# Storing two 64 MB gradients from ScalarE's queue, behind VectorE, in place of GpSimd's queue

## The chip, the cores and the metric

The kernel runs on one core of one Trainium2 chip. Its time is device microseconds of that core, from the start of the program to its end. A core has five engines with a queue of instructions each, and each queue runs in order: TensorE (PE; its weight loads are PEld), VectorE (DVE), ScalarE (ACT), GpSimd (POOL) and SyncE (SP). SP, ScalarE and GpSimd can issue DMA transfers between the chip's memory (HBM) and the core's on-chip buffers (SBUF, PSUM); 16 DMA engines carry them out.

## The reference: what is computed

One decode step of a small transformer block with a cache, forward and backward, B = 2 sequences, D = 640, H = 32 heads of width 128, a cache of 4096 positions, all in bfloat16:

```
h   = x + attention(layernorm(x), k_cache, v_cache) @ wo      # softmax over 4096 positions, per head
out = h + relu(layernorm(h) @ w1) @ w2                        # Dff = 1728
gradients of out (with grad_out) to x, k_cache, v_cache, wq, wo, w1, w2
```

k_cache and v_cache are (2, 32, 4096, 128): 64 tiles of 1 MB each, 128 partitions of 8 KB. Their gradients have the same size. For one head (b, h) with scores p (softmax), query q, gradient `go` of the head's output, and `dp` = V go, they are outer products: gV[s, :] = p[s] go and gK[s, :] = p[s] (dp[s] - p.dp) q scale. So 128 MB are written for gK (out_2) and gV (out_3), and V is read twice.

## The kernel before, in words

**Two passes over the heads.** The first pass (`p1_iter`) runs over the 64 heads and reads K and V of each: PE transposes K's tile group by group (`t_ps`, two banks), ScalarE copies each group out (`t_sb`, line 429), PE multiplies it with the query (scores), ScalarE takes the exponential (`ep`, line 524), VectorE weights K by it (`pk`, line 470), and PE forms M = pk' V (line 460). The second pass (`p2_iter`) runs over the heads again in the order `turns` and reads V as `Wt` (twelve V tiles are kept from the first pass): PE transposes it, ScalarE copies, PE forms `dp`; ScalarE scales the rows `rb` (go and q of this head, line 882); VectorE writes gV (two halves, line 844, from `rb` and `pp`), `gsp` from dp (line 858), and gK (two halves, line 844). For 19 heads ScalarE writes the last eight of gV's 32 column groups (line 930). gV and gK are stored by one DMA each: lines 909 and 931 for gV, 899 and 941 for gK. All four issue from GpSimd's queue.

**Steps.** `p2_iter` is a generator; each `next` of it is a step, some five to eight for a head. The main loop (`for n, (i, j) in enumerate(plan)`) takes steps of `p2_iter` between the steps of `p1_iter` while the first pass runs (i is not None; a head of the second pass for every second of the first, from i = 41 on), and later one step after the other, with background work between them (`bg_step`: gradients of the weights, their outer products `ot`, the sums `gxj`). Everything is issued in the order in which Python calls it; there is no other scheduler. Each engine's queue holds its own share of that order.

**Buffers.** 1 MB tiles come from a fixed set of buffers with owners ("ld" for loads, "g" for gK and gV, "f" and "q" for others). `take` gets one, `give` returns it in program order; the next user then waits on the chip for the last reader of the buffer, for a gK or gV that is its store's landing. Loads go out on SP's queue through `pump` as soon as an "ld" buffer has been given.

**Semaphores.** In the built program the DMAs of SP and ScalarE signal eight semaphores in turn, so that each waits for the landing of the eighth before it; the DMAs of GpSimd have eight of their own.

Of the kernel before, what the change touches and what calls it, by code (L numbers as in the profile page):

```python
# [15 lines left out]
def kernel(  # L16
# [20 lines left out]
    nc = tc.nc  # L37
# [402 lines left out]
    def natural(cache, b, h):  # L440
        return cache[b, h].rearrange("(p sc) d -> p sc d", sc=NSC)
# [412 lines left out]
    def score_grad(j, c):  # L854
# [5 lines left out]
            in1=P_bf[:, b * H + h, :, None].to_broadcast([128, NSC, 2]), op0=ALU.add, op1=ALU.mult)  # L860
        return gsp

    def p2_iter(j, busy, act=0, own_gK=False, early=False):

        c = S2[j] if j < NP1 else None
        p = S2.get(j - 1)
        if p is not None:
            bp, hp = turns[j - 1]
            last_dp(j - 1, p)
            gsp = score_grad(j - 1, p)  # L870
        if c is not None:
            b, h = turns[j]
            go = gom[:, h, b, :, :]

            bank = pst([128, 512], FP32, "sps", "dp_ps")
            for k, col in enumerate((goc, qsc)):
                nc.tensor.matmul(bank[:, 128 + k * 128:256 + k * 128],  # L877
                                 lhsT=col[:, h, b:b + 1].to_broadcast([128, 128]), rhs=ident_bf[:],
                                 start=True, stop=True)
            c["dp"] = bank[:, 0:NSC]  # L880
            rb = mats.tile([128, 256], BF16, tag="rb", bufs=3, name="rb")
            nc.scalar.activation(out=rb[:], in_=bank[:, 128:384], func=ACT.Copy, scale=rt[:, b, h:h + 1])  # L882
            pp = small.tile([128, NSC, 2], BF16, tag="pp", bufs=2, name="pp")
            nc.gpsimd.tensor_copy(out=pp[:], in_=P_bf[:, b * H + h, :, None].to_broadcast([128, NSC, 2]))
            c.update(rb=rb, pp=pp)
            if act:
                pa = small.tile([128, 8], FP32, tag="pa", bufs=2, name="pa")
                nc.gpsimd.tensor_copy(out=pa[:], in_=P_bf[:, b * H + h, NSC - act:NSC])
            c["T0"] = pair_transpose(c["W"], 0, busy=busy)
        if p is not None:  # L890
            gK = take("g", [128, NSC, 128], "gK")
            outer_half(gK, p["rb"][:, 128:256], gsp, 0)
        yield
        if early:
            gV = take("g", [128, NSC, 128], "gV")
            outer_half(gV, c["rb"][:, 0:128], c["pp"], 0)
        if p is not None:
            outer_half(gK, p["rb"][:, 128:256], gsp, 1)
            nc.gpsimd.dma_start(out=natural(out_2, bp, hp), in_=gK[:])  # L899
            give(gK)  # L900
            del S2[j - 1]
        yield
        if c is None:
            return
        c["T1"] = pair_transpose(c["W"], 1, busy=busy)
        pair_matvec(c["dp"], c.pop("T0"), 0, go)
        if early:
            outer_half(gV, c["rb"][:, 0:128], c["pp"], 1)
            nc.gpsimd.dma_start(out=natural(out_3, b, h), in_=gV[:])
        yield  # L910
        c["T2"] = pair_transpose(c["W"], 2, busy=busy)
        pair_matvec(c["dp"], c.pop("T1"), 1, go)
        yield
        c["T3"] = pair_transpose(c["W"], 3, busy=busy)
        give(c["W"], "g" if j < H and j != 1 and owned["g"] < 3 else None)
        pair_matvec(c["dp"], c.pop("T2"), 2, go)
        if early:
            give(gV)
            yield
            last_dp(j, c)  # L920
            gsp = score_grad(j, c)
        else:
            gV = take("g", [128, NSC, 128], "gV")
            outer_half(gV, c["rb"][:, 0:128], c["pp"], 0)
            yield
            if own_gK:
                last_dp(j, c)
            outer_half(gV, c["rb"][:, 0:128], c["pp"], 1, act)
            for k in range(act):
                nc.scalar.activation(out=gV[:, NSC - act + k, :], in_=c["rb"][:, 0:128], func=ACT.Copy, scale=pa[:, k:k + 1])  # L930
            nc.gpsimd.dma_start(out=natural(out_3, b, h), in_=gV[:])  # L931
            give(gV)
            if own_gK:
                gsp = score_grad(j, c)
            yield
        if own_gK:
            gK = take("g", [128, NSC, 128], "gK")
            outer_half(gK, c["rb"][:, 128:256], gsp, 0)
            yield
            outer_half(gK, c["rb"][:, 128:256], gsp, 1)  # L940
            nc.gpsimd.dma_start(out=natural(out_2, b, h), in_=gK[:])
            give(gK)
            del S2[j]
            yield

# [267 lines left out]
    def p2_step():  # L1213
        nonlocal g2
        try:
            next(g2)
        except StopIteration:
            g2 = None

    for n, (i, j) in enumerate(plan):  # L1220
        all_go = all(("go", B - 1, h) in done for h in range(H))
        if i is None and plan[n - 1][0] is not None:
            pkp.release()
            big1 = tc.alloc_tile_pool(name="big1", bufs=1)
            for _ in range(2):
                more_home("ld", big1)
            share(ld=KEPT[1] + 4, g=5)
        if all_go and not late[0]:
            wop.release()
            big3 = tc.alloc_tile_pool(name="big3", bufs=1, side="right")  # L1230
            for tag in ("ld", "g", "g", "q", "q", "q"):
                more_home(tag, big3)
        late[0] = all_go
        more = int(late[0])
        if fin is not None and not bg2 and not bg3:
            share(ld=8 + 3 * more, g=7 + 3 * more)
        elif fin is not None and j >= H + KEPT[1] - 1:
            share(ld=5 + more, g=6 + 2 * more, f=3, q=2 + 3 * more)
        if j is not None:
            while g2 is not None:  # L1240
                p2_step()
            if j < NP1:
                bg_until(("go", *turns[j]))
            g2 = p2_iter(j, 0, 8 if i is None and j <= H else 0, i is not None and plan[n + 1][1] is None, j < EARLY)
        if i is None and ("w1", 1) in done and fin is None:
            wts.release()
            fin = tc.alloc_tile_pool(name="fin", bufs=1)
            big2 = tc.alloc_tile_pool(name="big2", bufs=1)
            more_home("f", big2)
            banks.update(sps=[2, 3], o=[4, 5, 6])  # L1250
            bg2.append(("fin", fin_gen(fin)))
            bg3.append(("gx", gx_gen(fin)))
        if i == 12:
            bg.append(("ga", ga_gen()))
        if i == H + 2:
            banks["bc"].insert(0, banks["sps"].pop(0))
        elif i == P2_AT:
            banks["bc"].remove(7)
            banks["sps"].insert(0, banks["bc"][0])
            banks["bc"] = [7]  # L1260
        rate = RATES[0 if i is not None and i <= H + 1 else 1 if j is None and i < P2_AT else
                     2 if i is not None else 3 if j <= H else 4]
        if i is None:
            spread[0] = 2
            at_k[0] = 1
            k = 0
            while g2 is not None:
                p2_step()
                pump()
                slot[0] = int(k in ((1, 3, 5) if j <= H else (1, 4)))  # L1270
                k += 1
                bg_step(0, rate)
                bg_step(1, RATE2 * (0.4 if spreading[0] else 1.0))
                bg_step(2, RATE3)
            continue
        at = MIXED if j is not None else REST
        for k, _ in enumerate(p1_iter(i, i < H + 1, 0)):
            for _ in range(at.get(k, 0)):
                if g2 is not None:
                    p2_step()  # L1280
            if k == 5 and not H + 2 < i < P2_AT + 6:
                a_heads(i)
            pump()

            spread[0] = 1 if i < P2_AT else 2
            at_k[0] = k
            if i >= P2_AT:
                slot[0] = int(k == 6 or (k == 1 and j is not None))
            elif i > H + 1:
                slot[0] = {1: 2, 3: 1, 4: 1, 6: 1}.get(k, 0)  # L1290
            else:
                slot[0] = int(k in (1, 6))
            bg_step(0, rate)
            bg_step(1, 0.0)
        if i is not None and i in (H + 1, NP1 + 1):
            bg.append((f"m{i // H - 1}", middle_gen(i // H - 1)))
    forced[0] = True
    slot[0] = 99
    left = [q for q in (bg, bg3, bg2) if q]
# [38 lines left out]
```

## Time and profile before

| | |
|---|---|
| median of 3 runs | 891.21 us (891.13 to 893.05) |
| profiled execution | 888.48 us, span 886.3 us |
| PE, PEld, DVE, ACT, POOL busy | 738.8, 618.2, 681.3, 498.8, 204.1 us |
| moved | 361.85 MB: 211.11 read, 149.13 written, the rest instructions and the like; mean 408 GB/s |
| gV and gK | 64 stores each of 1024 KB on POOL's queue, median 14.9 and 15.0 us from issue to landing |

The span is from the first to the last instruction. The profile cuts it into 40 slices of 22.16 us, counted here from 0. First pass alone: to about 260 us. Both passes: to about 460. Second pass alone with the rest: to the end. "DMA share" is the busy share of the 16 DMA engines; "landing" is from the issue of a transfer to the semaphore that tells of its completion. The chain is the work that ended last, followed back from the end. A window's line gives its length, the busy time of the engines, the clock granted to PE, the DMA share and GB/s.

### The profile page before, as it was taken

Reading aid. Unit: us, or ns where it says so; the run is one execution under the profiler, and the core shown is the slowest. Engines: PE = TensorE matmul, PEld = TensorE weight load, DVE = VectorE, ACT = ScalarE, POOL = GpSimd, SP = SyncE. Lnnn points to the kernel's source line nnn. Section 1 sums busy time; section 2 is a strip of 40 time slices with the busy share of each in tenths; the row PEclk is TensorE's granted clock in tenths of the full one; section 3 lists DMA queues with packets and bytes.
Section 4 is the critical chain, followed back from the end, with each engine's and each line's share of the span. In section 5 each row is a group of like instructions: output and inputs, shape, how many; then the busy total and the mean of one; then the engine's idle time right before and its main releaser. Section 6 shows DMA issues by size and latency. Waiting matters only on the chain.

```text
span 886.3 us, 24732 instructions
## 1 busy us (share of the span) xinstructions
PE 738.8 (83%) x10143; PEld 618.2 (70%) x10143; DVE 681.3 (77%) x1281; ACT 498.8 (56%) x1292; POOL 204.1 (23%) x358
## 2 busy tenths in 40 slices
PE   4999899999999997988868767787877899867690
PEld 4887788888887886877757656665656667564550
DVE  2666787877788896876778887878788689989861
ACT  1444343446776664654536767777656766545570
POOL 1344433343312010000011332222222111111220
PEclk9999999999999999998995655555566755555555
DMA  9999999999879999999999999999999999999996
GB/s 380 423 420 414 417 409 417 425 423 412 332 295 402 423 423 426 422 426 425 414 398 396 418 421 421 420 413 420 419 416 403 417 425 420 425 425 425 425 424 275
DMA packets 56289, 361.85 MB, mean 408 GB/s; under 512 B 5680, under 2 KB 11760, under 8 KB 15472
## 3 DMA queue, kind: packets, MB, share of 16 engines
q1 hardware_dynamic: 34520, 211.13, 57.8%
q0 software_dynamic: 18432, 134.23, 36.5%
q10 hardware_dynamic: 3224, 14.92, 4.1%
q8 instruction: 80, 1.31, 0.5%
q14 instruction: 33, 0.27, 0.1%
HBM read 211.11 MB, written 149.13 MB: 406 GB/s over the span
## 4 chain that ended last, share of the span: by engine, by line
PE 35%; DMA 34%; DVE 16%; ACT 7%; issue 5%; SPq 0%; POOL 0%; ACTq 0%; POOLq 0%; DVEq 0%
DMA Vt<-in_A_v_cache_dram 15%; PE t_ps L424 14%; DMA out_dram<-gK 11%; PE m_ps L460 9%; DVE gK L844 4%; DVE gV L844 4%; DMA out_dram<-gV 3%; ACT gV L930 3%; PE s_ps L437 3%; DMA wqs<-in_A_wq_dram 3%; DVE pk L470 2%; PE u_ps L498 2%; ACT t_sb L429 2%; PE dp_ps L437 2%; DVE gxj L678 2%
## 5 line engine op out<-in xcount | busy, mean ns | idle before, releaser
L429 ACT COPY t_sb<-t_ps 128x512 f32<-128x512 f32 x479 | 273.1, 587 | 192.4 <-PE t_ps L424 188.6
L437 PEld LDWEIGHTS <-t_sb 128*128 128x128 bf16 x4096 | 178.9, 102 | 63.8 <-ACT t_sb L429 36.2
L424 PE MATMUL t_ps<-ident_f,Wt 128*128 128x128 f32 x832 | 198.6, 389 | 0.9 <-ACT t_sb L429 0.9
L470 DVE TENSOR_TENSOR pk<-Kt,ep 128x2048 bf16<-128x2048 bf16 (+1 forms) x128 | 152.6, 1193 | 47.1 <-ACT ep L524 29.0
L460 PE MATMUL m_ps<-pk,Vt 128*128 128x129 bf16 x2048 | 172.0, 223 | 19.9 <-DMA Vt<-in_A_v_cache_dram 18.8
L844 DVE TENSOR_TENSOR gK<-rb,gsp 128x2048 bf16<-128x2048 bf16 x128 | 153.4, 1227 | 13.3 <-DMA out_dram<-gV 8.5
L460 PEld LDWEIGHTS <-Vt 128*128 128x128 bf16 x2048 | 125.6, 99 | 50.2 <-issue 28.4
L424 PEld LDWEIGHTS t_ps<-ident_f,Wt 128*128 128x128 f32 x832 | 138.2, 202 | 31.9 <-issue 25.2
L424 PE MATMUL t_ps<-ident_f,Kt 128*128 128x128 f32 x1024 | 156.0, 286 | 2.5 <-DMA Kt<-in_A_k_cache_dram 1.9
L844 DVE TENSOR_TENSOR gV<-rb,pp 128x2048 bf16<-128x2048 bf16 (+1 forms) x128 | 142.7, 1139 | 16.3 <-DMA out_dram<-gK 9.9
L486 POOL COPY pk<-ep 128x16 bf16<-128x16 bf16 x80 | 83.6, 1046 | 158.4 <-ACT ep L524 80.0
L424 PEld LDWEIGHTS t_ps<-ident_f,Kt 128*128 128x128 f32 x1024 | 113.9, 145 | 5.0 <-ACT t_sb L429 2.7
L437 PE MATMUL dp_ps<-gom,t_sb 128*128 128x2 bf16 x2048 | 96.0, 168 | 25.1 <-ACT t_sb L429 24.7
L931 POOL DMA_DIRECT2D out_dram<-gV x62 | 33.0, 533 | 305.3 <-DVE gsp L858 135.1
L437 PE MATMUL s_ps<-qm,t_sb 128*128 128x2 bf16 x2048 | 87.4, 164 | 1.5 <-DVE t_sb L427 1.5
L986 ACT CAST ot<-o_ps 128x512 bf16<-128x512 f32 (+3 forms) x152 | 67.5, 491 | 8.4 <-DMA out_dram<-ot 5.2
L588 ACT CAST MT<-m_ps 128x128 bf16<-128x128 f32 x64 | 17.0, 266 | 94.5 <-PE m_ps L460 94.4
L899 POOL DMA_DIRECT2D out_dram<-gK x53 | 28.2, 533 | 135.4 <-DVE gK L844 104.9
L882 ACT ACTIVATE rb<-dp_ps,rt 128x256 bf16<-128x256 f32 x64 | 30.2, 472 | 44.7 <-PE dp_ps L877 43.4
L678 DVE CUSTOM_DVE_ANT_0 hbc<-wo_t,hbc 128x640 bf16<-128x640 bf16 x64 | 52.8, 825 | 0.3
L678 DVE CUSTOM_DVE_ANT_0 gxj<-wqs,gqr 128x1024 bf16<-128x1024 bf16 x40 | 48.7, 1217 | 1.0 <-DMA wqs<-in_A_wq_dram 0.8
L930 ACT ACTIVATE gV<-rb,pa 128x128 bf16<-128x128 bf16 x152 | 46.5, 392 | 3.9 <-DMA out_dram<-gK 3.9
(205 smaller groups left out, 758.2 us busy)
## 6 DMA issues: line engine op xcount, KB each, us to landing
Kt<-in_A_k_cache_dram SPq DMA_DIRECT2D x64, 1024.0 KB, 19.4
Vt<-in_A_v_cache_dram SPq DMA_DIRECT2D x64, 1024.0 KB, 15.5
out_dram<-gV POOLq DMA_DIRECT2D x64, 1024.0 KB, 14.9
out_dram<-gK POOLq DMA_DIRECT2D x64, 1024.0 KB, 15.0
Wt<-in_A_v_cache_dram SPq DMA_DIRECT2D x52, 1024.0 KB, 11.6
wq_t<-in_A_wq_dram SPq DMA_DIRECT2D x5, 1024.0 KB, 7.8
wo_t<-in_A_wo_dram SPq DMA_DIRECT2D x4, 1280.0 KB, 17.6
wqs<-in_A_wq_dram SPq DMA_DIRECT2D x5, 1024.0 KB, 22.3
```

The costliest lines, as they stand in the source:

```text
L424: nc.tensor.transpose(t_ps[:, j, :], natf[:, 2 * cc:2 * cc + 2, :].rearrange("p c k -> p (c k)"), ident_f[:])
L429: nc.scalar.copy(out=t_sb[:], in_=t_ps[:])
L437: nc.tensor.matmul(dst[:, sc:sc + 2], lhsT=v[:, j, :, par], rhs=vecs[:, par, :], start=(par == 0), stop=(par == 1))
L460: nc.tensor.matmul(r["m"][:, 0:129], lhsT=r["V"][:, sc, :], rhs=r["pk"][sc // HALF][:, sc % HALF, 0:129], start=(sc == 0), stop=(sc == NSC ...
L470: nc.vector.tensor_tensor(out=p["pk"][k][:, 0:n, 0:128].rearrange("p s (a two) -> p s a two", two=2), in0=p["K"][:, sl, :].rearrange("p s ...
L486: nc.gpsimd.tensor_copy(out=col, in_=e)
L678: nc.vector.tensor_tensor_reduce(out=junk[0:kc, 0:width], in0=in0, in1=in1, scale=1.0, scalar=0.0, op0=ALU.mult, op1=ALU.add, accum_out=acc)
L844: nc.vector.tensor_tensor(out=pairs_view(dst[:, sl, :]), in0=row.rearrange("p (a two) -> p a two", two=2)[:, None, :, :].to_broadcast([128 ...
L882: nc.scalar.activation(out=rb[:], in_=bank[:, 128:384], func=ACT.Copy, scale=rt[:, b, h:h + 1])
L930: nc.scalar.activation(out=gV[:, NSC - act + k, :], in_=c["rb"][:, 0:128], func=ACT.Copy, scale=pa[:, k:k + 1])
L931: nc.gpsimd.dma_start(out=natural(out_3, b, h), in_=gV[:])
L986: nc.scalar.copy(out=ot[0:P, k, n0:n0 + nn], in_=o_ps[0:P, 0:nn])
```

## The change

All gK and gV are stored from ScalarE's queue. `store` puts a store on a list with a count; `send`, called after each step of `p2_iter`, counts down and issues those whose count has run out, and only then gives the buffer back. The count is 1 while the first pass still runs (the store is issued after the next step) and 2 from the point where the second pass runs alone (`alone`). The two earliest heads gave gV's buffer back at a later step; now `send` does it. After the loop the last stores are sent. The order of instructions on PE, DVE and SP stays as it was; 128 DMA issues leave POOL's queue and stand in ACT's, which held 21.

```diff
+    unsent = []
+    alone = [False]
+    LAG = 2
+
+    def store(out_ap, t):
+
+        unsent.append([LAG if alone[0] else 1, out_ap, t])
+
+    def send(all_of_them=False):
+
+        for entry in list(unsent):
+            entry[0] -= 1
+            if entry[0] < 0 or all_of_them:
+                nc.scalar.dma_start(out=entry[1], in_=entry[2][:])
+                give(entry[2])
+                unsent.remove(entry)
+
     def p2_iter(j, busy, act=0, own_gK=False, early=False):
...
             outer_half(gK, p["rb"][:, 128:256], gsp, 1)
-            nc.gpsimd.dma_start(out=natural(out_2, bp, hp), in_=gK[:])
-            give(gK)
+            store(natural(out_2, bp, hp), gK)
             del S2[j - 1]
...
             outer_half(gV, c["rb"][:, 0:128], c["pp"], 1)
-            nc.gpsimd.dma_start(out=natural(out_3, b, h), in_=gV[:])
+            store(natural(out_3, b, h), gV)
...
         if early:
-            give(gV)
             yield
...
-            nc.gpsimd.dma_start(out=natural(out_3, b, h), in_=gV[:])
-            give(gV)
+            store(natural(out_3, b, h), gV)
...
-            nc.gpsimd.dma_start(out=natural(out_2, b, h), in_=gK[:])
-            give(gK)
+            store(natural(out_2, b, h), gK)
...
             next(g2)
         except StopIteration:
             g2 = None
+        send()
...
         if i is None:
+            alone[0] = True
...
+    send(True)
     forced[0] = True
     slot[0] = 99
```

## The prediction

> **What bounds the kernel now.** I read the page's slices and queues first, then the waits, the two store lines, the windows table for the stretches that stand out, and last the chain. The slices say where the transfers leave room; the queues say what one MB costs on each.
>
> ```profile
> DMA  9999999999879999999999999999999999999996
> GB/s 380 423 420 414 417 409 417 425 423 412 332 295 402 423 423 426 422 426 425 414 398 396 418 421 421 420 413 420 419 416 403 417 425 420 425 425 425 425 424 275
> ...
> q1 hardware_dynamic: 34520, 211.13, 57.8%
> q0 software_dynamic: 18432, 134.23, 36.5%
> q10 hardware_dynamic: 3224, 14.92, 4.1%
> ```
>
> The DMA engines are full in 37 of 40 slices. 361.85 MB at the 425 GB/s of the best slices is 851 us of the 886.3 us span; the other 35 us are the low numbers: slices 10 and 11 (counted from 0; the first store of gV goes out at 261.98, near the end of 11), 19 to 21, 0.2 to 1.1 us in each of slices 22 to 30, and the tail. A change that moves no byte can gain or lose only there, or by the price of a packet. q0 is GpSimd's queue (all gK and gV), q1 SP's loads, q10 ScalarE's stores of `ot`.
>
> The rows of the two kinds of store, and the two largest waits of the stores:
>
> ```profile
> L931 POOL DMA_DIRECT2D out_dram<-gV x62: 531/533/533, 297.1 to 865.0; - x62
> ...
> DMA to landing us min/median/max: 7.3/14.9/36.3
> ```
>
> ```profile
> L989 ACTq DMA_DIRECT2D out_dram<-ot x19: 338/343/703, 567.7 to 865.3; - x19
> ```
>
> ```profile
> POOL out_dram L931 <- DVE gsp L858: 135.1, 18, 14.4
> POOL out_dram L899 <- DVE gK L844: 104.9, 37, 8.5
> ```
>
> The reader is to see that GpSimd spends its time waiting for VectorE at each store, which costs nothing there, and what an issue takes on either queue: 0.533 us on GpSimd, 0.343 us on ScalarE.
>
> Two stretches in 5 us windows (columns: PE, PEld, DVE, ACT, POOL busy; clock; DMA share; GB/s):
>
> ```profile
> 260.00:265.00 5.00, 4.94 (x87) 4.34 (x80) 4.02 (x8) 2.73 (x8) 0.69 (x1) 1.00 0.42 151
> 265.00:270.00 5.00, 5.00 (x90) 4.19 (x87) 4.64 (x8) 4.34 (x16) 2.21 (x3) 1.00 0.96 347
> ```
>
> ```profile
> 471.00:476.00 5.00, 4.03 (x41) 3.55 (x40) 4.55 (x11) 4.24 (x12) 1.28 (x4) 0.50 0.97 382
> 476.00:481.00 5.00, 4.39 (x42) 3.79 (x40) 4.55 (x18) 3.61 (x11) 0.42 (x1) 0.50 1.02 388
> 481.00:486.00 5.00, 4.21 (x92) 4.08 (x93) 3.42 (x4) 3.45 (x9) 2.15 (x4) 0.50 0.99 378
> ```
>
> Here the engines, not the transfers, set the pace: 382, 388 and 378 GB/s against 425. The chain confirms it for the second one (it runs over DVE gK, gV, ACT gV and PE t_ps from 466 to 489), and shows two stores that gate a buffer:
>
> ```profile
> 454.46 10.21 DMA out_dram<-gV
> ...
> 776.81 36.45 DMA out_dram<-gK
> ```
>
> **The change, part by part.** (1) *Issue time.* GpSimd loses 128 issues x 0.533 = 68.2 us of its 204.1; ScalarE gains 128 x 0.343 = 43.9 us on 498.8, 56% to 61% of the span. Where the transfers are full this is hidden behind them: with about five transfers of 1.05 MB under way (14.9 us to landing over 2.47 us each, 1.05 MB at 425) a ScalarE that is later by under 12 us starves nobody. If that cover went, 43.9 us is the upper end. It is gone in the two stretches above. In the first, stores at 261.98 and 269.05 fall before 270, from where GB/s is 415 or more: 2 x 0.343 = 0.7 us. In the second there are seven, from 468.62 to 489.02; there ScalarE's next copy often starts as the one before it ends (474.36, two copies in 1.05), so each issue is on the way of the PE t_ps - ACT t_sb exchange: 7 x 0.343 = 2.4 us. From 531 to 612 the chain again runs over PE t_ps and ACT gV, so the engines lose about 0.34 to 0.69 us per head there, some ten heads, 3.4 to 6.9 us; the gK issued at 612.40 is 18.4 us under way (the chain), so the queue behind it covers that: 0.
>
> (2) *Order on ScalarE.* Its queue is in order, so a store waits there for VectorE and all copies behind it wait too; PE waits for those copies (t_ps) and VectorE for PE (gsp). I laid each store's place in the order of the built instructions beside the times of before. In the first pass:
>
> ```profile
> 300.29 1.07 ACT L429 COPY t_sb<-t_ps 128x512 f32<-128x512 f32 x2 [0.35 <-PE t_ps L424]
> ...
> 300.51 1.21 DVE L844 TENSOR_TENSOR gK<-rb,gsp 128x2048 bf16<-128x2048 bf16 x1
> ...
> 302.01 0.53 POOL L941 DMA_DIRECT2D out_dram<-gK  x1 [4.38 <-DVE gK L844]
> ```
>
> The gK store now stands ahead of the two copies at 300.29 and waits until 301.72: 1.4 us late plus the issue, 1.2 to 2.3 us in each of nine heads up to 435, about 16 us of ScalarE. The cover: every few heads PE waits for a Vt that is 17 to 21 us under way (the chain at 330, 380, 418), at 423 to 426 GB/s. The engines run ahead and then wait, so I cost it at 0; without cover it would be 16 us. From 468 on stores are two steps behind, and up to 620 their place mostly comes 0.2 to 2.9 us after VectorE's end, so ScalarE does not wait, but the store goes out that much later and its buffer comes back later. With five under way that shortens the queue, not the rate: 0. In 468 to 489 VectorE waits for a buffer once (0.75 us at 469.76); I count that inside the 2.4.
>
> (3) *Semaphores.* In the built order each transfer of SP and ScalarE waits until the eighth before it has landed; GpSimd's stores had eight of their own. So at most 8 are under way instead of 16. Only the last third had more: 36.45 us at 776 is 36.45/2.47 = 14.8 transfers. Eight still fill 19.8 us: 0 for the rate, a rival below for the end. On SP, loads are queued behind such a wait; they are asked for several heads ahead.
>
> (4) *GpSimd freed.* Its pp and pa copies no longer stand behind a store; the chain passes one of them once for 0.07 us. 0.
>
> (5) *Packet price.* Per MB the queues take 36.5/134.23 = 0.272% (q0), 57.8/211.13 = 0.274% (q1), 4.1/14.92 = 0.275% (q10). The nearest row, q10, is stores by the same queue: 134.23 x 0.003% = 0.4%, 3.4 us dearer, up to 7.5 us with its rounding (4.15), -0.5 us with 4.05. The other end: slices 22 to 30 run at 403 to 421 GB/s with a full DMA share; against 425 their deficits (74 GB/s in all, of 425, times 22.16 us) add up to 3.9 us, and if the software queue makes all of it, the change gains 3.9; with slices 19 to 21 (67 more) 7.4. I take 0, between them, since q0, q1 and q10 differ by less than rounding.
>
> The sum: 0.7 + 2.4 = 3.1 us. The profiled execution took 888.48 us (span 886.3 and 2.2 around it), so it would take 891.6; it lies 2.7 us below the median of 891.21, and for the median I forecast 894.3.
>
> The Trainium skill (DMA: Bandwidth & Descriptors, Latency and other measured facts) puts the first byte at about 0.6 us on the hardware path and 1 us on GpSimd's. That would bring each buffer back 0.4 us sooner; on the five stores of 446 to 463, where VectorE waits for them, it is an estimated 2 us, and the sum 892.3. The trace does not bear it out: the fastest landing is 7.3 us on GpSimd and 9.2 on ScalarE's queue (under more load).
>
> **Rivals.** *A. Forecast*, as summed: 893 to 897.
> *B. All hidden.* Even the 2.4 us fall into waits for PE: 891.2. For it: ScalarE is idle 44% of the span; against: the exchange at 474 has no slack.
> *C. The software queue is what costs 1 to 5% in slices 22 to 30.* For it: each head there has one load and two stores through q0, and the first pass, with less of q0, runs at 422 to 426 (slices 13 to 18). Against: SP's last load of Wt goes out by 811, so that slices 37 and 38 are stores alone, at 425 and 424; and `ot` packets through ScalarE show no better price. If transfers and not engines are then the pace of the whole stretch, A's loss is not seen, and the time is 891.2 - 3.9 = 887.3, with slices 19 to 21 down to 883.8. It is faster once more than 1.8 us of it come true. The Trainium skill (the same page, SWDGE vs HWDGE vs iDMA) says that GpSimd writes its descriptors into SBUF, where VectorE's two-port modes lock it out, and that the hardware path is immune. By that rule C is what happens, at 887.3; slices 32 to 35, at 420 to 425 with VectorE busy for 8 tenths or more, speak against its weight.
> *D. Eight semaphores throttle the last third.* The engines may lead the transfers by 8 x 2.47 us instead of 14.8 x 2.47: they are held up by up to 16.8 us at 776. It decides if they can't make that up: PE is busy 20.53 of 22.10 us just before the end,
>
> ```profile
> 842.00:864.10 22.10, 20.53 (x141) 12.51 (x140) 14.96 (x16) 16.09 (x32) 4.64 (x9) 0.50 1.01 425
> ```
>
> and the last store goes out at 869.7. Held up in full, it would go at 886.5, land 6.8 us later (the shortest gK) and end the span near 895 (1.7 us follow): +8.7, 899.9. Against: a full queue means that no transfer time is lost, and the last store now has 16.6 us between issue and end of span, which takes up some of it.
>
> **How the numbers follow.** A 0.40, B 0.20, C 0.28, D 0.12. A tells itself from no change by little: 0.2% (1.8 us) is about what a measurement of this kernel tells, and A is 3.1. Faster: C and a little of B, 0.30. Same: the rest of B and the low end of A, 0.22. Slower: 0.48. A's own range is 893 to 897. C lies between 883.8 and 887.3, nearer to the second, D at 899.9: 885.5 to 900 holds A, B, most of C and most of D. What is left out is C with all of slices 19 to 21, a D that is not taken up, and a packet price 7.5 us up.
>
> **What would show it.** Right: ScalarE's line for gK and gV at about 0.34 us x128, waits of ScalarE for DVE gK below 435 of some 1 to 2 us each, GB/s of slices 19 to 21 at or below 414, 398 and 396, slices 13 to 18 unchanged at 422 to 426. C: slices 22 to 30 at 424, q10 at 0.267% per MB or less. D: DMA share under 0.95 after slice 30, landings of at most 20 us, PE idle for ACT before the end. What would make me wrong: a stall of ScalarE in the first pass that the Vt waits do not take up (slices 13 to 18 under 420), worth up to 16 us; or loads that start so much later behind the shared semaphores that the queue runs dry.

## The result, and the profile after

Before: 890.3 us (median, 887.12 to 893.05). Changed: 893.5 us (889.01 to 898.3). The ratio is 1.0046, 95% interval 1.0026 to 1.0066: slower by 4.1 us of 890.3 (the two medians differ by 3.2), where 894.3 us and +3.1 us were forecast. The profiled execution took 893.85 us, with a span of 892.0 us (before: 888.48 and 886.3).

From the page of the changed kernel, the slices and the queues:

```profile
DMA  9999999999989999999999999999999999999997
GB/s 379 423 420 415 416 403 417 426 422 399 338 312 374 423 424 424 424 425 425 401 377 381 424 422 423 398 411 419 417 411 394 424 426 423 427 427 419 412 377 325
...
q1 hardware_dynamic: 34520, 211.13, 58.0%
q10 hardware_dynamic: 21656, 149.14, 40.3%
```

The slices of this page are 22.3 us long. GB/s fall in slice 12 (402 before, 374 now), in slices 20 and 21, from 446 to 491 us (398 and 396 before, 377 and 381 now), a little in slices 25, 26 and 30 (398, 411, 394), and at the end, where 425, 425, 424 have become 419, 412, 377. The queues' price is unchanged: 40.3% of 892.0 us over 149.14 MB is 2.41 us per MB on ScalarE's queue, and 36.5% of 886.3 us over 134.23 MB was 2.41 on GpSimd's.

The new store line, and ScalarE's waits that it brings (engine, line, what it waited for: us in all, times, longest):

```profile
L876 ACTq DMA_DIRECT2D out_dram<-gV x64: 338/338/1569, 262.1 to 879.2; - x64
L876 ACTq DMA_DIRECT2D out_dram<-gK x64: 338/338/1608, 270.8 to 882.9; - x64
...
DMA to landing us min/median/max: 5.2/12.4/21.9
```

```profile
ACT t_sb L429 <- DVE gK L844: 14.7, 7, 2.7
ACT ot L999 <- DMA out_dram<-gK: 9.1, 3, 7.4
ACT t_sb L429 <- PE dp_ps L894: 7.0, 4, 2.1
```

The first and the third row are the wait in the first pass that the prediction laid out. At the place that it named, the gK store at 302.09 holds the two copies back. The profile puts this one down to PE's `dp_ps` (third row), but VectorE ends gK at 302.06, just before the store goes out.

```profile
300.72 0.17 ACT L589 COPY OU<-m_ps 128x1 f32<-128x1 f32 x1
...
300.85 1.21 DVE L844 TENSOR_TENSOR gK<-rb,gsp 128x2048 bf16<-128x2048 bf16 x1
...
302.09 0.34 ACTq L876 DMA_DIRECT2D out_dram<-gK  x1
302.47 1.07 ACT L429 COPY t_sb<-t_ps 128x512 f32<-128x512 f32 x2 [1.58 <-PE dp_ps L894]
```

The second row is new: a store stands on ScalarE until another transfer has landed, and the copies behind it stand too. In the timeline the store of 720.01 waits for the eighth transfer before it, the gK store of 699.97, which lands at 719.93 after 20 us, and PE waits over 8 us:

```profile
699.97 0.34 ACTq L876 DMA_DIRECT2D out_dram<-gK  x1
...
720.01 0.34 ACTq L876 DMA_DIRECT2D out_dram<-gV  x1
720.39 0.75 ACT L999 CAST ot<-o_ps 128x512 bf16<-128x512 f32 x2 [7.36 <-DMA out_dram<-gK]
721.02 0.26 PE L993 MATMUL o_ps<-gh1r,OFr 2*128 2x128 bf16 x1 [8.09 <-ACT ot L999]
```

And one row that the prediction did not price at all, in VectorE's waits from 255 to 290 us. Before, this wait is not there:

```profile
DVE gK L844 <- DMA out_dram<-gV: 1.7, 1, 1.7
```

To see where a kernel loses time I cut each profiled execution by bytes moved, summed from the packets of its trace: us that each stretch took, up to the last packet of a load or store and on to the end of the span (the last three columns: the end, the last VectorE operation, and MB issued but not yet moved, mean of 770 to 780 us). The kernels below the first two are those of the experiments. One execution each, so a difference under 1 us says little. The execution of alone_late is the longest of its runs.

```
MB moved      0-85  -115  -178  -205  -285  -320  -last  end   span   last DVE  lead
before       205.3  84.2 148.5  67.2 192.2  82.7 104.0   2.1  886.3    869.4   9.3
after        205.6  85.1 148.6  69.6 193.9  82.3 105.5   1.5  892.0    882.8   3.9
lag_only     205.5  85.4 149.0  67.7 192.6  82.4 103.9   2.1  888.7    873.6   9.1
lag_late     205.5  82.9 148.6  67.1 192.0  82.7 104.6   2.1  885.5    867.2   9.9
late_give    205.3  83.4 148.9  68.4 193.7  82.5 106.5   1.5  890.3    881.2   3.8
first_late   205.3  83.1 148.6  68.6 191.6  82.8 104.4   5.4  889.8    868.7   9.0
alone_late   205.3  84.6 148.6  68.6 194.3  82.4 108.0   1.3  893.1    884.1   3.9
copy_late    205.4  84.1 148.7  68.4 191.8  82.7 105.7   2.1  888.9    875.1   7.7
last_pool    205.3  82.4 148.5  67.8 193.0  82.4 105.7   3.2  888.4    869.1   9.6
gk_pool      205.2  82.6 148.5  67.7 193.4  82.8 105.0   3.8  889.1    877.0   2.6
```

After against before: 0.9 us more from 85 to 115 MB (about 205 to 290 us), 2.4 from 178 to 205 MB (about 438 to 508), 1.7 from 205 to 285, 1.5 near the end, less 0.6 behind the last packet.

### The profile page after: what moved, and what is told of

Same layout as the page of the kernel before. It is cut to its first block, busy times and chain, and to the rows that moved or that the text cites. A ratio compares the mean times of both kernels' runs of the same rounds, so it can differ in the third digit from the quotient of the medians.

```text
span 892.0 us, 24707 instructions
## 1 busy us (share of the span) xinstructions
PE 742.5 (83%) x10143; PEld 620.2 (70%) x10143; DVE 681.0 (76%) x1281; ACT 497.5 (56%) x1292; POOL 144.9 (16%) x230
## 3 DMA queue, kind: packets, MB, share of 16 engines
q10 hardware_dynamic: 21656, 149.14, 40.3%
## 5 line engine op out<-in xcount | busy, mean ns | idle before, releaser
L424 PE MATMUL t_ps<-ident_f,Wt 128*128 128x128 f32 x832 | 200.9, 393 | 2.5 <-ACT t_sb L429 2.4
L460 PE MATMUL m_ps<-pk,Vt 128*128 128x129 bf16 x2048 | 172.5, 223 | 15.6 <-DMA Vt<-in_A_v_cache_dram 14.4
L901 POOL COPY pp<-P_bf 128x64 bf16<-128x64 bf16 x64 | 40.5, 634 | 504.1 <-DVE gV L844 495.1
L486 POOL COPY pk<-ep 128x16 bf16<-128x16 bf16 x80 | 84.6, 1059 | 157.8 <-ACT ep L524 80.9
L858 DVE SCALAR_TENSOR_TENSOR gsp<-dp_ps,negdot,P_bf 128x64 bf16<-128x64 f32 x64 | 18.0, 281 | 51.6 <-PE dp_ps L437 51.4
L899 ACT ACTIVATE rb<-dp_ps,rt 128x256 bf16<-128x256 f32 x64 | 30.3, 473 | 23.7 <-PE dp_ps L894 16.9
## 6 DMA issues: line engine op xcount, KB each, us to landing
out_dram<-gK ACTq DMA_DIRECT2D x64, 1024.0 KB, 11.4
```

What stands on the lines that cost most here:

```text
L424: nc.tensor.transpose(t_ps[:, j, :], natf[:, 2 * cc:2 * cc + 2, :].rearrange("p c k -> p (c k)"), ident_f[:])
L460: nc.tensor.matmul(r["m"][:, 0:129], lhsT=r["V"][:, sc, :], rhs=r["pk"][sc // HALF][:, sc % HALF, 0:129], start=(sc == 0), stop=(sc == NSC ...
L486: nc.gpsimd.tensor_copy(out=col, in_=e)
```

## Experiments

Three theories stood at the start. Issue time: ScalarE's time and place in the order cost it (the forecast). Delay: buffers come back later. Shared semaphores: stores and loads wait for each other, so the engines cannot run ahead (rival D). Ratios are to the kernel before, measured beside each run on the same chip. The first four kernels below ran on one chip, the next four on a second, the last four on a third.

**lag_only.** The delay alone, from GpSimd's queue.

```diff
-                nc.scalar.dma_start(out=entry[1], in_=entry[2][:])
+                nc.gpsimd.dma_start(out=entry[1], in_=entry[2][:])
```

> Stores with the change's delay, but from GpSimd's queue. Measured so far: before 890.3, changed 893.5 (ratio 1.0046, +4.1 us). Issue time on ScalarE (the forecast): the loss is gone, ratio 1.000 +- 0.002. Buffers that come back later (the delay): the loss stays, 1.004. Shared semaphores: gone, 1.000, and the lead of the issued stores over the transfers after 700 us grows to 8 MB or more again, as before, in place of 3 to 4 MB.

Measured: 1.0021 (1.0004 to 1.0037). About half of the loss is there without ScalarE. That is between the 1.004 of "delay" and the 1.000 of the other two, and within the 0.002 that "issue time" allowed, so it decides little. The lead is back (9.1 MB), as "shared semaphores" said.

**lag_copy.** ScalarE's place in the order without its semaphores.

```diff
-                nc.scalar.dma_start(out=entry[1], in_=entry[2][:])
+                nc.scalar.copy(out=entry[2][:, NSC - 1, :], in_=entry[2][:, NSC - 1, :])
+                nc.gpsimd.dma_start(out=entry[1], in_=entry[2][:])
```

> As lag_only, and at each place where the changed kernel issues a store ScalarE copies the last 128x128 group of the tile onto itself (0.39 us, the output stays the same); the store then goes out from GpSimd. So ScalarE waits for VectorE in the same places and loses 0.39 us instead of 0.343 us each time, but the semaphores are those of before. Issue time and order on ScalarE: the full loss, 1.004 to 1.005. Delay: 1.004. Shared semaphores: 1.000 to 1.002, lead over the transfers 8 MB or more after 700 us, no ScalarE wait of over 3 us for a landing.

Measured: 1.0151 (1.0127 to 1.0174), three times what any theory gave. Its timeline shows 7.4 us of it:

```profile
265.16 0.69 POOL L877 DMA_DIRECT2D out_dram<-gV  x1 [8.95 <-ACT pk L488]
267.74 0.28 DVE L858 SCALAR_TENSOR_TENSOR gsp<-dp_ps,negdot,P_bf 128x64 bf16<-128x64 f32 x1 [0.36 <-PE dp_ps L437]
275.39 1.22 DVE L844 TENSOR_TENSOR gK<-rb,gsp 128x2048 bf16<-128x2048 bf16 x1 [7.37 <-DMA out_dram<-gV]
```

The first gK is written into the buffer of the first gV, and waits for that store to land. It is the row of 1.7 us in the changed kernel, 3.2 in lag_only, none before. The stretch from 85 to 115 MB takes 94.1 us here (84.2 before).

**first_only, alone_only.** One half of the change each; in the other half the store goes out at once from GpSimd.

```diff
     def store(out_ap, t):
+        if alone[0]:                  # alone_only: if not alone[0]
+            nc.gpsimd.dma_start(out=out_ap, in_=t[:])
+            give(t)
+            return
```

> ScalarE's queue with one step of delay while the first pass runs; GpSimd's queue without delay where the second pass runs alone. Issue time: 0.7 us from 262 to 270 and part of the 2.4 us (stores before 460), 1.000 to 1.002. Delay of two steps: gone, 1.000. Shared semaphores: 1.000, lead over the transfers as before (up to 9.75 MB near 780 us).

> GpSimd's queue without delay while the first pass runs; ScalarE's queue with two steps of delay where the second pass runs alone. Issue time: 2.4 us or a little less, 1.002 to 1.003. Delay: 1.004. Shared semaphores: the loss stays, 1.003 to 1.005; lead over the transfers 3 to 4 MB after 700 us, DMA share under 1 after 840 us.

Measured: first_only 1.0043 (1.0027 to 1.0058), alone_only 1.0088 (1.0059 to 1.0117). Together the halves cost more than the whole (1.0046), and alone_only loses 4.5 us to the same wait of gK at 268 us, in a stretch whose queue is that of the kernel before. So neither half was cleanly undone: both had kept a fourth part of the change.

**The fourth part.** In the kernel before, the two earliest heads store gV and call `give(gV)` two steps later, after `give(c["W"], "g")`. `take` hands out the buffer that was given first. In the changed kernel `send` gives gV's buffer back right behind its store, ahead of W's; so the next gK takes the buffer that is still being stored and not W's, which is idle. Four kernels put this one thing back:

```diff
-    def store(out_ap, t):
+    def store(out_ap, t, keep=False):
...
-                give(entry[2])
+                if not entry[3]:
+                    give(entry[2])
...
-            store(natural(out_3, b, h), gV)          # the early heads
+            store(natural(out_3, b, h), gV, True)
...
         if early:
+            give(gV)
             yield
```

late_give is the changed kernel with it, lag_late is lag_only, first_late first_only, alone_late alone_only.

> The changed kernel, but the two earliest heads hand gV's buffer back where the kernel before does (two steps after the store), so that the free list gives gK another buffer. Order of the free buffers: the wait of VectorE for the landing of gV near 266 us (1.7 us in the changed kernel's profile, 4.5 and 7.4 us in alone_only and lag_copy, none before) is gone, and the ratio falls by 0.2 to 0.5%, to 1.000 to 1.003. Issue time (forecast) and shared semaphores: the ratio stays at 1.004 to 1.005.

> lag_only (GpSimd's queue with the delay, 1.0021) with the same later return of the two buffers. Order of the free buffers: 1.000. Delay by itself: stays at 1.002.

> first_only (1.0043) with the later return. Order of the free buffers alone: 1.000. Issue time and waits of ScalarE beside the first pass: the rest, 1.001 to 1.003. Shared semaphores: nothing, lead over the transfers up to 9 MB or more near 780 us.

> alone_only (1.0088) with the later return: GpSimd's queue as in the kernel before beside the first pass, ScalarE's with two steps of delay where the second pass runs alone. Order of the free buffers: about 0.5% less, 1.004. Shared semaphores: 1.003 to 1.005, from 320 MB moved to the end 108 to 111 us in place of 106.2, lead over the transfers at most 5 MB. Issue time: 1.002 to 1.003, lost between 178 and 205 MB moved.

| | as changed | buffer back later |
|---|---|---|
| ScalarE in both parts | 1.0046 (1.0026 to 1.0066) | late_give 1.0027 (1.0014 to 1.0040) |
| GpSimd with the delay | 1.0021 (1.0004 to 1.0037) | lag_late 0.9990 (0.9973 to 1.0007) |
| ScalarE beside the first pass | 1.0043 (1.0027 to 1.0058) | first_late 1.0026 (1.0007 to 1.0044) |
| ScalarE in the second pass alone | 1.0088 (1.0059 to 1.0117) | alone_late 1.0031 (1.0016 to 1.0046) |

All four fall, by 0.17 to 0.57%, and VectorE's wait is gone. In three of the pairs the intervals overlap; what shows the cause is that all four fall and that the time goes where the wait was. From 85 to 115 MB alone_only took 91.3 us and alone_late 84.6, lag_only 85.4 and lag_late 82.9, the changed kernel 85.1 and late_give 83.4; only first_only (83.2, a wait of 1.5 us) and first_late (83.1) differ by nothing there. late_give's row of the same operation has no bracket:

```profile
265.61 1.22 DVE L844 TENSOR_TENSOR gK<-rb,gsp 128x2048 bf16<-128x2048 bf16 x1
```

The delay by itself costs nothing that can be measured (lag_late). What is left, 0.27%, is ScalarE's queue. The clock granted to PE does not explain it: it was 0.773 on average over the runs of late_give and over those of the kernel before on that chip. The loss lies in the second pass alone, as far as the intervals tell: alone_late's 0.31% is as much as late_give's 0.27%. first_late's 0.26% does not contradict this. In its profile the transfers end at 884.4 us, as before (884.1), but the span ends 5.4 us later in place of 2.1, because GpSimd's drain behind its last store ends 4.6 us after the last packet and not 1.4; first_only's profile shows the same 4.6.

**copy_late, last_pool, gk_pool, sp_late.** What of ScalarE's queue costs: its time and order, or the semaphores? All four start from late_give.

```diff
# copy_late
-                nc.scalar.dma_start(out=entry[1], in_=entry[2][:])
+                nc.scalar.copy(out=entry[2][:, NSC - 1, :], in_=entry[2][:, NSC - 1, :])
+                nc.gpsimd.dma_start(out=entry[1], in_=entry[2][:])
# last_pool: entry[4] is set from head 41 on;  gk_pool: entry[4] is set for gK in the second pass alone
-                nc.scalar.dma_start(out=entry[1], in_=entry[2][:])
+                (nc.gpsimd if entry[4] else nc.scalar).dma_start(out=entry[1], in_=entry[2][:])
# sp_late
-                nc.scalar.dma_start(out=entry[1], in_=entry[2][:])
+                (nc.sync if alone[0] else nc.scalar).dma_start(out=entry[1], in_=entry[2][:])
```

> lag_copy (1.0151: ScalarE copies a 128x128 group of the tile onto itself where the changed kernel stores, the store follows from GpSimd) with the later return of the two early buffers. Of its 13 us, 7.4 are the wait for the early gV: without it 1.006 or 1.007. If ScalarE's place in the order and its 0.39 us are what costs (issue time): 1.004 or more, in all stretches. If only the shared semaphores cost: 1.000 to 1.001, which lag_copy already speaks against.

> late_give, but from head 41 of the second pass on (the last third, from about 690 us) all stores go out from GpSimd's queue with the same delay. Shared semaphores, whose price is at the end: from 320 MB moved to the last store's packet 104 us as in the kernel before (104.1), in place of 106.5 in late_give; ratio 1.000 to 1.0015. Issue time in the stretch from 468 to 489 us (forecast): that stretch is as in late_give, ratio stays at 1.002 to 1.003.

> late_give (1.0027), but where the second pass runs alone gK goes out from GpSimd's queue, with the same delay, and gV stays on ScalarE's; so the two kinds of store wait on different semaphores, 16 in all. Shared semaphores: the lead over the transfers grows to 6.5 MB or more near 780 us (3 to 4 MB in late_give), last VectorE end near 870 us in place of 881, ratio 1.000 to 1.001. Issue time on ScalarE: half of it stays, 1.0013 to 1.002, and the lead stays at 3 to 4 MB.

> late_give, but where the second pass runs alone the stores go out from SP's queue with the same delay: the same eight semaphores as the loads, and nothing of it on ScalarE; loads of SP stand behind stores. Shared semaphores: lead over the transfers at most 5 MB, DMA share under 1 after 840 us, 1.003 or more. Issue time and order on ScalarE: gone, 1.000 to 1.001.

copy_late: 1.0039 (1.0026 to 1.0053). ScalarE's time and order, with the semaphores of before, cost no less than late_give does; so they can be enough for the whole remaining loss. It is not the same load on ScalarE, though. The copies took less than supposed (0.301 us, the 0.39 us were of the slower line 930), 38.5 us in all, but for their tiles ScalarE waits 50.5 us, of which 35.2 come after 441 us; late_give's ScalarE waits some 21 us for VectorE there, and 24 for landings:

```profile
ACT gK L876 <- DVE gK L844: 33.0, 20, 6.1
ACT gV L876 <- DVE gV L844: 17.5, 13, 3.3
```

last_pool: 1.0014 (0.9999 to 1.0029). With GpSimd for the last third the lead is back (9.6 MB), the last VectorE operation is at 869.1 us as before and not at 881.2, and the DMA engines stay full. The windows of 842 to 864 us of the kernel before, late_give and last_pool (PE, PEld, DVE, ACT, POOL busy; clock; DMA share; GB/s):

```profile
842.00:864.00 22.00, 20.43 (x137) 12.40 (x136) 14.86 (x16) 16.09 (x32) 4.64 (x9) 0.50 1.01 425
```

```profile
842.00:864.00 22.00, 19.13 (x179) 13.04 (x178) 13.35 (x16) 15.15 (x32) 0.71 (x3) 0.66 0.87 360
```

```profile
842.00:864.00 22.00, 20.22 (x160) 12.78 (x160) 15.86 (x17) 17.21 (x34) 4.35 (x8) 0.59 1.01 424
```

So the queue does run short at the end when all stores are ScalarE's (0.87; in the changed kernel itself 0.97). Its price, late_give less last_pool, is 0.13%, and the two intervals overlap: about 1 us, not resolved. From 320 MB to the last packet last_pool still took 105.7 us, where 104 were expected and late_give took 106.5. Part of it is taken back at the end of the span again (3.2 us behind the last packet against 1.5).

gk_pool: 1.0055 (1.0033 to 1.0077), no better than late_give and perhaps worse (the intervals overlap), which no theory expected; the lead did not come back (2.6 MB). Sixteen semaphores in place of eight did not help: from 770 to 780 us, by the landings in its trace, GpSimd had 1.2 transfers issued and not landed, SP and ScalarE 4.6. In its timeline a store on ScalarE waits 9 us for a load of SP, which was issued at 704.36 and was 32 us under way:

```profile
736.64 0.34 ACTq L876 DMA_DIRECT2D out_dram<-gV  x1
737.02 0.75 ACT L1001 CAST ot<-o_ps 128x128 bf16<-128x128 f32 x2 [8.99 <-DMA Wt<-in_A_v_cache_dram]
```

sp_late: 1.0132 (1.0113 to 1.0150). It shows the wait from the other side. SP's waits from 700 to 740 us:

```profile
SPq L1081 <- DMA out_dram<-ot: 16.8, 1, 16.8
SPq L876 <- DMA out_dram<-ot: 11.9, 1, 11.9
```

The load of `wqs` stood from 702 to 719 us until a store of `ot` had landed that ScalarE issued only at 711.59. In the built order a transfer of SP or ScalarE waits for the eighth before it in the order of the program, on whichever of the two queues that is, issued or not. The transfers ran at 0.70 of their share meanwhile, and the stretch from 285 to 320 MB took 94.6 us in place of 82.7:

```profile
709.12:731.28 22.16, 20.67 (x170) 14.14 (x168) 13.72 (x18) 13.29 (x31) 0.24 (x1) 0.50 0.70 264
```

From 842 to 864 us, where a share under 1 was expected, it was 1.01. Because of these waits sp_late does not tell ScalarE's time from the semaphores. Two things stay open: why gk_pool is no faster than late_give (its profiled execution, 890.86 us, is the shortest of its runs, so the profile shows little of it), and how the loss of the second pass divides between ScalarE's time and the shorter lead, which copy_late (lead 7.7 MB, 1.0039) and last_pool bound but do not separate.

## Why the prediction was right, and where not

The time and the sign were right, +4.1 us against +3.1, and slower had been given the largest chance (0.48). That the sum fits so well is partly luck: it was 0.7 us too high in what it priced (2.4 measured) and left out a term of about 1.7 us.

- **Step 1, issue time, 3.1 us: near in size, its place and cause not separated.** With the buffer order put back, ScalarE's queue costs 2.4 us (late_give), and that holds its order and its semaphores too. From 262 to 270 us nothing is seen (0.7 forecast). From 178 to 205 MB, which holds the stretch from 468 to 489 us, late_give is 1.3 us over lag_late (2.4 forecast). From 205 to 285 MB it is 1.7 us over, where I had costed 3.4 to 6.9 us of lost engine time at 0, "the queue behind it covers that". last_pool, the same program up to about 690 us, is only 0.7 and 1.0 us over lag_late, so one execution each does not settle the split. The cover was thinner than the 12 us of the prediction: from 500 to 700 us late_give had 1.2 to 4.1 MB issued and not moved (means of 10 us), 2.8 on average, which is 6.6 us at 425 GB/s. That it failed in places is argued, not shown. "About five transfers" was a slip too: 14.9/2.47 is 6, and the trace of before has 5.5 issued and not landed on average from 510 to 700 us.
- **Step 2, order, about 16 us of waits at a cost of 0: right.** Up to 441 us ScalarE waits 11.4 us in five places for gK, and 7.0 us in four that the profile puts down to `dp_ps`: 18.4 us in nine places, where nine heads were forecast. The stretch from 115 to 178 MB takes 148.6 us, as before (148.5). Part of it is one wait in place of another: what `rb` waits for PE there fell from 16.9 to 7.0 us. The later return of buffers is free too (lag_late).
- **Step 3, semaphores, 0: the depth mis-sized, the price small.** "Eight still fill 19.8 us" took eight transfers under way as eight still to be moved. By the landings in the traces, 6.6 transfers were issued and not landed from 770 to 780 us (13.2 before), but of their bytes only 3.9 MB had not been moved (9.3 before): 9 us at 425 GB/s. The engines end 13.4 us later (882.8 against 869.4), not far from the 16.8 of rival D. But D's price of 8.7 us is not seen: the last store now has 7.6 us to its last packet and not 14.4, which was the argument against D. What remains is about 1 us, by last_pool, and that is not resolved.
- **Step 4, GpSimd freed, 0: slightly wrong.** Without GpSimd's stores the span ends 1.5 us after the last packet in place of 2.1, and the execution is 1.9 us longer than the span in place of 2.2: about 1 us gained. The 2 us that I estimated from the Trainium skill (DMA: Bandwidth & Descriptors, Latency and other measured facts), for buffers that come back 0.4 us sooner, are not seen: from 441 to 491 us VectorE waits 5.7 us for stores, and waited 6.3 before. (The prediction's 7.3 us for the fastest landing on GpSimd is that of line 931 alone; a gK took 6.8 and line 909's gV 6.0.)
- **Step 5, packet price, 0: right.** 2.41 us per MB on both queues, and slices 25 to 30 did not rise to 424. Rival C is out. The Trainium skill (DMA: Bandwidth & Descriptors, SWDGE vs HWDGE vs iDMA) has VectorE locking GpSimd out of writing its descriptors; what that would save does not show here.
- **The missing term: the order of the free buffers, 0.19% or 1.7 us** (1.0046 less 1.0027). The diff shows it, as a `give(gV)` that moves up by a step, and I read it as a buffer that comes back earlier and so as harmless. I asked when a buffer is given, and not which buffer the next `take` then gets. The 0.19% is the difference of two ratios whose intervals overlap, so its size is rough. The wait depends on when the first store lands: 1.5, 1.7, 3.2, 4.5 and 7.4 us in five profiles.

Rival B (all hidden, no loss) is out by the interval; but beside the first pass it is what happened.

## What to carry to other kernels

When a release of a buffer moves by one step, follow the free list: who takes that buffer next, and is it still being read? Here an earlier release cost about 1.7 us out of 4.1, because it came ahead of a release of an idle buffer. An issue of 0.34 us on an engine in lock step with another was hidden beside the first pass, where the transfers were 3.7 MB behind on average (late_give, 300 to 440 us), and it seems only partly hidden where they were 2.8 MB behind and at times 1.2, so read the depth of the queue stretch by stretch and not from its mean. Count it in bytes still to be moved: 6.6 transfers under way held 3.9 MB. And before moving stores to a queue that shares its semaphores with the loads, look at which transfer each of them will wait for in the order of the program: where the second pass runs alone, all stores on SP (1.0132) were clearly worse than all on ScalarE (1.0027), gK alone on GpSimd was no better (1.0055), and all on GpSimd in both parts with the same delay (0.9990) showed no loss against the kernel before.

## What the runs showed of the hardware that was not expected

A drain stands behind GpSimd's last store, and the program ends behind it. It ended 1.4 us after the last packet of all in the five kernels in which GpSimd issues all 128 stores (before, lag_only, lag_late, lag_copy, copy_late), 4.6 us in first_only and first_late (101 stores), and 2.4 and 2.6 us in last_pool and gk_pool (47 and 51). So kernels that mix the two kinds of queue, with GpSimd's stores last, ended up to 3.2 us later behind their transfers. alone_only and alone_late mix them too, but their 27 stores on GpSimd come first (the last goes out at 469 and 462 us); their drain ended 28 us before the last packet, and the span 1.3 us after it. What decides the time wasn't tried.

A store on ScalarE that waits for a load of SP (9 us in gk_pool), and a load on SP that waits for a store of ScalarE (16.8 us in sp_late), come from semaphores handed out in turn over both queues. The depth that this leaves from 770 to 780 us was 2.6 to 3.9 MB not yet moved in the kernels that store from ScalarE there, with 4.6 to 6.6 transfers of SP and ScalarE issued and not landed. The eight semaphores suggest 8 transfers of 1.05 MB.
